# A complex-decay recurrence before a mixture of experts: TensorE adds the carried state to a chunk's state product, and the decays are kept in three places

## The chip, the cores and the metric

The kernel runs on one core of one Trainium2 chip. The metric is device time of one execution in microseconds (us), the median of the runs of the same program. A profile is one more execution, taken by the hardware profiler; its span, from the first to the last instruction, is somewhat shorter than its own time.

## The reference

Every (batch, head) has a complex state S of 48 x 48 that decays row by row with a complex factor and takes one outer product per token; the output of the recurrence goes through a top-1 mixture of experts with a capacity.

```python
mag = np.sqrt(a_re * a_re + a_im * a_im)
scale = np.minimum(mag, 0.999) / (mag + 1e-06)
a_re_n, a_im_n = (a_re * scale, a_im * scale)
for t in range(S):                       # S = 768, B = 4, H = 8, D = 48
    new_re = ar * S_re - ai * S_im
    new_im = ar * S_im + ai * S_re
    S_re, S_im = (new_re + kv, new_im)   # kv = k[t] (outer) v[t]
    y[:, :, t] = np.einsum('bhd,bhde->bhe', q[:, :, t], S_re)
x = y.transpose(0, 2, 1, 3).reshape(B * S, H * D)
# MoE: 3072 tokens, 8 experts, 384 -> 1024 (relu) -> 384, out = gate * expert(x)
```

## The kernel before, in words

**Tiling.** The 768 tokens are cut into 8 chunks of 96, the chunks into 4 groups of 2. Three kinds of work run through each other until the experts begin.

- *Slices.* A group has 6 slices of 8 decay factors. `norm_slice` (L370; `norm_first`, L285, for the very first) turns the raw decays into normalised ones; `scan` (L466) multiplies them up step by step on VectorE, a multiplication (L493) and an addition (L498) for each of 8 steps; `post` (L512) makes from the products the scaled q and k (`qko`, L541, L576) and sends them to HBM (`scr`, L584 to L598).
- *Units.* A unit is one batch b and one chunk c, 8 to a group, and it works one group behind the slices. It loads the scaled rows back (`qkc`, L684), transposes them (`tr`, L710), multiplies q by k (`pa`, L726), masks (`a_sb`, L730), and makes the output (`y`, L788 within the chunk, L793 from the carried state `z`). It also makes the state for the next chunk: the product k times v (`s`, L737 to L742, in the one PSUM tile `s_all`), the addition of the carried state z (`add`, L744), the multiplication by the chunk's decay (L759, L762, L765), and two accumulating DMAs that swap halves (`swap`, L753), after which the next chunk's z is there.
- *Routing.* The gate and the places of the tokens, and the sending of rows to the experts (L1133).

After the last unit's rows are placed, the experts run (`ph` L1374, `my` L1382, L1397).

**Decays.** A slice's tile `a4` has four places for each step: before the scan they hold r, -i, i, r. `mr` (L448) writes r into place 0 and `mi` (L444) writes i into place 2 on VectorE; `ci` (L451) copies i, negated, to place 1 and `cr` (L458) copies r to place 3 on ScalarE. The scan's multiplication reads all four places in a row, and its addition writes the running product into places 0 and 1. In the first slice of a group one step starts the product, so there `ci` is in two pieces.

**Order.** All of this is recorded as operations of a planner (`Plan.op`, L60). It holds a duration, an engine, the operations it follows, the buffers and a wished time for each, places them one by one (`solve`, L78), and the instructions of every engine are then written in that order. An engine works strictly in its order, so the order decides who waits. `fill_gaps` (L158) puts idle matmuls (`keep`, L225; they write other columns of `s_all`) into TensorE's planned gaps of over 0.4 us. The state product and its addition stand in the plan as:

```python
o = plan.op(K("S"), "PE", .8, s, w + SLATE * f, after=loaded + [K("LF"), K("V")], bufs=[("s", "u", b, c), R("qkc"), R("v")])
d = plan.op(K("D"), "DVE" if c else "ACT", dve(384) if c else act(384), add, w + (SLATE + 1) * f, after=[o] + zready, ...)
```

There is one `s` buffer: the next unit's state product waits until the addition has read this one.

Of the kernel before, what the change touches and what calls it, by code (L numbers as in the profile page):

```python
# [38 lines left out]
class Op:  # L39

    def __init__(self, eng, dur, fn, after, bufs, want, kb, idx):
        self.eng, self.dur, self.fn, self.after, self.bufs, self.want, self.kb, self.idx = eng, dur, fn, after, bufs, want, kb, idx
        self.lat = None
        self.start = None
        self.form = None
        self.begun = False


class Plan:
# [108 lines left out]
    def fill_gaps(self, keep, begin, stop, least=.4, one=.23):  # L158

        out, end = [], 0.  # L160
        for o in self.order:
            if o.eng == "PE":
                gap = o.start - end
                if begin < end and o.start < stop and gap > least:
# [3 lines left out]
                end = o.start + o.dur  # L168
            out.append(o)
# [11 lines left out]
class Att:  # L181
# [74 lines left out]
    def tile_a4(self, g, j):  # L256
        if (g, j) not in self.a4:
            self.a4[g, j] = self.p_a4.tile([128, SL, 4, D], F32, tag="a4", name=f"a4_{g}_{j}", bufs=RINGS["a4"])
        return self.a4[g, j]
# [25 lines left out]
    def norm_first(self, s0):  # L285
# [14 lines left out]
        for p, h in enumerate(range(n - HALF, -1, -HALF)):  # L300
# [13 lines left out]
            def xb(i=i):  # L314
                nc.vector.tensor_tensor(out=st['a4'][:, i, 3, :], in0=st['a4'][:, i, 0, :], in1=st['a4'][:, i, 1, :], op=ALU.add)

            def xc(i=i):
                nc.scalar.activation(st['ln'][:, i], st['a4'][:, i, 3, :], AF.Ln, bias=self.b_tiny)
# [9 lines left out]
            def mm(i=i):  # L328
                nc.vector.tensor_tensor(out=st['ln'][:, i], in0=st['a4'][:, i, 3, :], in1=st['ln'][:, i], op=ALU.mult)
# [14 lines left out]
            def mr(i=i):  # L344
                nc.vector.tensor_tensor(out=st['a4'][:, i, 0, :], in0=st['a'][:, 0, i], in1=st['t5'][:, i], op=ALU.mult)

            def ci(i=i, p=p):
                k = i.stop - (p == 0)
                nc.scalar.mul(out=st['a4'][:, i.start:k, 1, :], in_=st['a4'][:, i.start:k, 2, :], mul=-1.0)
                if p == 0:  # L350
                    nc.scalar.copy(out=st['a4'][:, k, 1, :], in_=st['a4'][:, k, 2, :])

            def cr(i=i):
                nc.scalar.copy(out=st['a4'][:, i, 3, :], in_=st['a4'][:, i, 0, :])  # L354
# [11 lines left out]
            orr = plan.op(None, "DVE", dve(m), mr, v + 7, after=[o], bufs=[a_, t5_, a4_])  # L366
            plan.op(K + ("i", p), "ACT", act(m) + .08 * (p == 0), ci, v + 7.5, after=[oi], bufs=[a4_])
            plan.op(K + ("r", p), "ACT", act(m), cr, v + 7.5, after=[orr], bufs=[a4_])

    def norm_slice(self, g, j, s0):  # L370
# [89 lines left out]
        oi = plan.op(None, "DVE", dve(n * D), mi, w + 10, after=[o], bufs=[a_, t5_, a4_])  # L460
        orr = plan.op(None, "DVE", dve(n * D), mr, w + 10.5, after=[o], bufs=[a_, t5_, a4_])
        plan.op(K + ("i",), "ACT", act(n * D) + .08 * (j == 0), ci, w + 11, after=[oi], bufs=[a4_])
        plan.op(K + ("r",), "ACT", act(n * D), cr, w + 11, after=[orr], bufs=[a4_])


    def scan(self, g, j, wants):  # L466
# [9 lines left out]
        for s in range(n - 1, -1, -1):  # L476
# [10 lines left out]
            def mul(cs, s=s, st=st, prev=prev):  # L487
# [1299 lines left out]
```

## Time and profile before

| | |
|---|---|
| median of 3 runs | 600.95 us (598.43 to 601.08) |
| profiled execution, its own time | 601.24 us |
| its span | 599.4 us |
| PE (TensorE matmul) busy | 530.0 us, 88% |
| DVE (VectorE) busy | 467.7 us, 78% |
| ACT (ScalarE) busy | 401.1 us, 67% |
| POOL (GpSimd) busy | 276.2 us, 46% |
| mean granted TensorE clock | 0.95 of full |

Shares are averages over two very different stages: slices and units up to some 366 us, and the experts from 372.6 us to the end, in which TensorE runs without a pause. Times of events are from the start of the span. A fp32 matmul stands in the trace as two records. A row's mean duration of one instruction is longer than what it takes of its engine, since the next one starts before it has ended; where work is dense the distance between two starts is what counts.

### The profile page before, as it was taken

Reading aid. Unit: us, or ns where it says so; the run is one execution under the profiler, and the core shown is the slowest. Engines: PE = TensorE matmul, PEld = TensorE weight load, DVE = VectorE, ACT = ScalarE, POOL = GpSimd, SP = SyncE. Lnnn points to the kernel's source line nnn. Section 1 sums busy time; section 2 is a strip of 40 time slices with the busy share of each in tenths; the row PEclk is TensorE's granted clock in tenths of the full one; section 3 lists DMA queues with packets and bytes.
Section 4 is the critical chain, followed back from the end, with each engine's and each line's share of the span. In section 5 each row is a group of like instructions: output and inputs, shape, how many; then the busy total and the mean of one; then the engine's idle time right before and its main releaser. Section 6 shows DMA issues by size and latency. Waiting matters only on the chain.

```text
span 599.4 us, 15649 instructions
## 1 busy us (share of the span) xinstructions
PE 530.0 (88%) x5453; PEld 460.3 (77%) x5453; DVE 467.7 (78%) x1388; ACT 401.1 (67%) x1115; POOL 276.2 (46%) x354
## 2 busy tenths in 40 slices
PE   2363879999999998999879998999999999999992
PEld 1131558777787776778768997999999999999991
DVE  5899979999899999999865668555797657567631
ACT  7656779998999889998564653345564746566430
POOL 9531414532457944476352722004554737355502
PEclk9667889999999999999997999999999999999997
DMA  5575797996898989879598972494745765884401
GB/s 172 179 192 159 179 225 179 266 235 164 207 233 202 233 240 227 219 195 204 139 183 191 252 197 48 72 228 140 168 128 127 213 152 174 189 206 139 128 19 39
DMA packets 90023, 105.51 MB, mean 176 GB/s; under 512 B 29846, under 2 KB 80495, under 8 KB 89936
## 3 DMA queue, kind: packets, MB, share of 16 engines
q1 hardware_dynamic: 72432, 57.27, 40.4%
q0 software_dynamic: 17504, 47.15, 29.9%
q8 instruction: 45, 0.74, 0.5%
q14 instruction: 42, 0.34, 0.2%
HBM read 71.41 MB, written 29.22 MB: 168 GB/s over the span
## 4 chain that ended last, share of the span: by engine, by line
PE 54%; ACT 18%; DVE 13%; DMA 8%; POOL 4%; issue 2%; POOLq 0%; SPq 0%; ACTq 0%; DVEq 0%
PE ph L1374 18%; PE my L1382 14%; PE my L1397 4%; ACT z L762 4%; PE pa L726 3%; DMA qkc<-scr 3%; DMA scr<-qko 3%; PE tr L710 2%; DVE xy L493 2%; PE y L788 2%; PE p L273 2%; PE n L273 2%; PE y L793 1%; DVE a L498 1%; DVE qko L576 1%
## 5 line engine op out<-in xcount | busy, mean ns | idle before, releaser
L1315 POOL DMA_INDIRECT out_dram<-oq,xr x66 | 69.5, 1054 | 61.4 <-ACT oq L1331 46.2
L1421 ACT ACTIVATE hh<-ph 128x448 fp32r<-128x448 f32 (+7 forms) x64 | 32.6, 510 | 96.6 <-PE ph L1374 96.6
L1422 DVE SCALAR_TENSOR_TENSOR hl<-ph,hh 128x448 fp32r<-128x448 f32 (+7 forms) x64 | 37.1, 580 | 66.5 <-ACT hh L1421 66.5
L1269 DVE TENSOR_TENSOR lo<-raw,hi 128x384 fp32r<-128x384 f32 (+2 forms) x128 | 65.4, 550 | 3.5 <-ACT hi L1268 3.2
L1374 PE MATMUL ph<-xh,hi 128*128 128x448 f32 (+7 forms) x192 | 67.3, 351 | 0.6 <-ACT xh L1227 0.6
L1374 PE MATMUL ph<-xh,lo 128*128 128x448 f32 (+7 forms) x192 | 67.2, 350 | 0.0
L1133 POOL DMA_INDIRECT disp<-x,idx x32 | 45.1, 1410 | 43.6 <-DVE a_sb L730 11.8
L755 POOL DMA_DIRECT2D z<-sx x56 | 47.4, 1060 | 31.6 <-ACT z L762 10.5
L493 DVE TENSOR_TENSOR xy<-a 128x192 f32<-128x192 f32 (+1 forms) x205 | 61.2, 313 | 0.6 <-ACT a L354 0.2
L710 PE MATMUL tr<-ident,qkc 81*96 81x81 f32 x512 | 54.0, 240 | 7.4 <-DMA qkc<-scr 4.1
L1268 ACT CAST hi<-raw 128x384 fp32r<-128x384 f32 (+2 forms) x128 | 58.9, 509 | 0.0
L273 PE MATMUL n<-a,ident 128*128 128x384 f32 x92 | 43.3, 604 | 16.8 <-ACT a L397 8.7
L726 PE MATMUL pa<-qT,kT 128*96 128x96 f32 x512 | 55.9, 255 | 0.8 <-ACT kT L714 0.8
L710 PEld LDWEIGHTS tr<-ident,qkc 81*96 81x96 f32 x512 | 41.6, 128 | 17.5 <-issue 5.5
L726 PEld LDWEIGHTS pa<-qT,kT 128*96 128x96 f32 x512 | 50.0, 169 | 2.8 <-ACT kT L714 1.4
L273 PE MATMUL p<-qko,ident 128*128 128x384 f32 x80 | 36.1, 580 | 16.5 <-ACT qko L530 16.4
L1382 PE MATMUL my<-hh,hi 128*128 128x448 f32 (+5 forms) x144 | 50.6, 351 | 0.0
L1382 PE MATMUL my<-hh,lo 128*128 128x448 f32 (+5 forms) x144 | 50.5, 351 | 0.0
L1382 PE MATMUL my<-hl,hi 128*128 128x448 f32 (+5 forms) x144 | 50.5, 351 | 0.0
L498 DVE TENSOR_TENSOR a<-xy 128x96 f32<-128x96 f32 (+1 forms) x221 | 49.1, 234 | 0.3
L730 DVE TENSOR_TENSOR a_sb<-pa,mask 96x384 f32<-96x384 f32 x64 | 34.9, 546 | 14.7 <-PE pa L726 14.6
L1374 PE MATMUL ph<-xl,hi 128*128 128x448 f32 (+7 forms) x192 | 46.2, 349 | 0.0
(248 smaller groups left out, 1442.6 us busy)
## 6 DMA issues: line engine op xcount, KB each, us to landing
qkc<-scr SPq DMA_DIRECT2D x32, 480.0 KB
raw<-in_moe_w_dram SPq DMA_DIRECT2D x128, 96.0 KB
raw<-in_moe_w_dram SPq DMA_DIRECT2D x32, 384.0 KB
scr<-qko POOLq DMA_DIRECT2D x44, 192.0 KB
scr<-qko POOLq DMA_DIRECT2D x20, 384.0 KB
a<-in_av_dram POOLq DMA_DIRECT2D x18, 384.0 KB
qkin<-in_xv_dram POOLq DMA_DIRECT2D x18, 384.0 KB
v<-in_vp_dram SPq DMA_DIRECT2D x32, 144.0 KB
```

The source lines that it names most:

```text
L273: nc.tensor.matmul(out=pt[:, :m], lhsT=self.ident, rhs=t[:, h:h + m], start=i == 0, stop=i == 1)
L493: nc.vector.tensor_tensor(out=st['xy'][:, :, cs].rearrange("p (u z) d -> p u z d", u=2), in0=a4[:, s, :, cs].rearrange("p (u z) d -> p u z ...
L498: nc.vector.tensor_tensor(out=self.a4[g, j][:, s, 0:2, cs], in0=xy[:, 0:4:2, cs], in1=xy[:, 1:4:2, cs], op=ALU.add)
L710: nc.tensor.transpose(out=pt[:, h * C:h * C + NE], in_=qk[:NE, 4 * hh + h, z_ * C:z_ * C + C], identity=self.ident[:NE, :NE])
L726: nc.tensor.matmul(out=pa[:, h * C:h * C + C], lhsT=kT[:, 4 * hh + h], rhs=qT[:, 4 * hh + h], start=True, stop=True)
L755: nc.gpsimd.dma_start(out=zn[a.start:a.stop or C], in_=st['sx'][o], accum_op=ALU.add)
L1133: ins = nc.gpsimd.indirect_dma_start(out=self.disp, out_offset=bass.IndirectOffsetOnAxis(ap=idx[:, c:c + 1], axis=0), in_=self.row(b, c0 + ...
L1268: return (lambda: nc.scalar.copy(out=h, in_=r), lambda: nc.vector.tensor_tensor(out=l, in0=r, in1=h.bitcast(F32), op=ALU.subtract))
L1269: lambda: nc.vector.tensor_tensor(out=l, in0=r, in1=h.bitcast(F32), op=ALU.subtract))
L1315: ins = nc.gpsimd.indirect_dma_start(out=out, out_offset=bass.IndirectOffsetOnAxis(ap=at, axis=0), in_=o, in_offset=None, bounds_check=las ...
L1374: nc.tensor.matmul(out=ph[:, :W], lhsT=a[:, k, fs], rhs=r[:, k, :W], start=i == 0, stop=i == len(parts) - 1)
L1382: nc.tensor.matmul(out=py[m][:, :W], lhsT=a[:, f % self.PF, ms], rhs=r[:, :W], start=f == 0 and i == 0, stop=f == NF - 1 and i == 2)
```

## The change

1. **State product.** For the units of chunks 1 to 5 (`summed`: 20 of the 28 units that make a state) TensorE leaves the product's accumulation open and a further matmul (`carry`) multiplies the carried z, 96 x 384, by the identity into the same PSUM tile. The sum is then only copied out, by ScalarE, where before VectorE added. Chunk 0 (copied by ScalarE before, too) and chunk 6 (added by VectorE) stay.
2. **No idle matmuls into an open sum.** `fill_gaps` puts none between a product and its carry.
3. **Three places.** `a4` holds -i, r, i. The multiplication reads (r, -i) and (i, r) out of them with a step of minus one place and writes the product over r and i. The copy `cr` is gone, and `ci` is in one piece. The readiness of a slice is that of `mr` and `ci`.

```diff
@@ Plan.fill_gaps
-                if begin < end and o.start < stop and gap > least:
+                if begin < end and o.start < stop and gap > least and not open_:
...
                 end = o.start + o.dur
+                open_ += o.opens
@@ tile_a4
-            self.a4[g, j] = self.p_a4.tile([128, SL, 4, D], F32, tag="a4", ...)
+            self.a4[g, j] = self.p_a4.tile([128, SL, 3, D], F32, tag="a4", ...)
@@ norm_slice (norm_first likewise)
-            nc.vector.tensor_tensor(out=self.a4[g, j][:, 0:n, 0, :], in0=st['a'][:, 0], in1=st['t5'], op=ALU.mult)
+            nc.vector.tensor_tensor(out=self.a4[g, j][:, 0:n, 1, :], in0=st['a'][:, 0], in1=st['t5'], op=ALU.mult)
         def ci():
-            a4 = self.a4[g, j]
-            k = n - (j == 0)
-            nc.scalar.mul(out=a4[:, 0:k, 1, :], in_=a4[:, 0:k, 2, :], mul=-1.0)
-            if j == 0:
-                nc.scalar.copy(out=a4[:, k, 1, :], in_=a4[:, k, 2, :])
-        def cr():
-            nc.scalar.copy(out=self.a4[g, j][:, 0:n, 3, :], in_=self.a4[g, j][:, 0:n, 0, :])
+            nc.scalar.mul(out=self.a4[g, j][:, 0:n, 0, :], in_=self.a4[g, j][:, 0:n, 2, :], mul=-1.0)
...
-        plan.op(K + ("r",), "ACT", act(n * D), cr, w + 11, after=[orr], bufs=[a4_])
+        plan.op(K + ("r",), "DVE", dve(n * D), mr, w + 10.5, after=[o], bufs=[a_, t5_, a4_])
@@ scan
-                w = self.a4[prev[0], prev[1]][:, prev[2], 0:2, cs]
+                w = self.a4[prev[0], prev[1]][:, prev[2], 1:3, cs]
...
+                a = a4[:, s, 1, cs]
+                a = bass.AP(a.tensor, a.offset, [a.ap[0], (D, 2), (-D, 2), a.ap[-1]])
                 nc.vector.tensor_tensor(out=st['xy'][:, :, cs].rearrange("p (u z) d -> p u z d", u=2),
-                                        in0=a4[:, s, :, cs].rearrange("p (u z) d -> p u z d", u=2), in1=w, op=ALU.mult)
+                                        in0=a, in1=w, op=ALU.mult)
@@ unit
-                                     start=True, stop=True)
+                                     start=h == 0 or not summed, stop=not summed)
+        summed = 0 < c and g < NG - 1
+        def carry():
+            nc.tensor.matmul(out=st['ps'], lhsT=self.ident[:, :C], rhs=z.rearrange("p h e -> p (h e)"), start=False, stop=True)
...
-            if c == 0:
+            if c == 0 or summed:
                 nc.scalar.copy(out=ss, in_=psv)
...
+            if summed:
+                o.opens = 1
+                o = plan.op(None, "PE", .68, carry, w + (SLATE + .5) * f, after=[o] + zready, bufs=[("s", "u", b, c), ("z", b, c)])
+                o.opens = -1
+            by = "DVE" if c and not summed else "ACT"
```

The planner places everything anew, so rows move on every engine. Two places matter to the prediction. The first is an inner unit, batch 2 of chunk 2. On VectorE, before, its addition (L751) stood among the slices' work (`a_2_3` is slice 3 of group 2, `qko_1`, `qko_2` are its slices 1 and 2, `sx` the state multiplied by a decay):

```order
L576 TENSOR_TENSOR qko_1_2393<-a_2_1_1724,v_2_1_2468 128x8x96
L449 TENSOR_TENSOR a_2_3_2174<-a_3_2004,t5n_3_2256 128x8x48
L1119 CAST idx_0_2559<-slot_0_2504 96x1
L751 TENSOR_TENSOR s_2_2660<-s_all,z_129 96x384
L765 TENSOR_TENSOR sx_1_1942<-s_1_1941,pcol_109 96x384
L765 TENSOR_TENSOR sx_2_2661<-s_2_2660,pcol_109 96x384
L493 TENSOR_TENSOR xy_3_7_2679<-a_2_3_2174,a_2_2_1916 128x192
```

VectorE has no such row any more for this unit (24 rows of this kind before, 4 after). TensorE now has, two transposes behind the unit's product (L730), the carry (L736):

```order
L1015 MATMUL x_1_2509<-ident,xt_1_2474 96x128 x4
L730 MATMUL s_all<-v_120,qkc_117 32x48 x24
L699 MATMUL tr_2_0_0_2550<-ident,qkc_117 96x81 x4
L699 MATMUL tr_2_1_0_2564<-ident,qkc_117 96x81 x4
L736 MATMUL s_all<-z_129,ident 96x384
L699 MATMUL tr_2_0_1_2575<-ident,qkc_117 96x81 x4
L699 MATMUL tr_2_1_1_2589<-ident,qkc_117 96x81 x4
```

and ScalarE the copy (L743), between two copies of transposed rows:

```order
L691 COPY qT_122<-ends_133 96x8x15
L743 COPY s_2_2586<-s_all 96x384
L703 COPY qT_122<-tr_2_0_1_2575 96x4x81
L703 COPY kT_124<-tr_2_1_1_2589 96x4x81
L519 ACTIVATE qko_2_2603<-a_2_2_1960 128x8x96
L756 ACTIVATE z_128<-s_2_2586,pcol_109 96x48 x8
```

The second place is on TensorE where the last group's units begin (batches 0 and 1 of chunk 6; `qkc_116` and `qkc_117` are their loaded rows, `y_6` the output of batch 0). Before:

```order
L710 MATMUL tr_6_1_1_4895<-ident,qkc_116 96x81 x4
L726 MATMUL pa_6_0_4903<-qT_122,kT_124 96x96 x4
L710 MATMUL tr_6_0_0_4920<-ident,qkc_117 96x81 x4
L726 MATMUL pa_6_1_4926<-qT_122,kT_124 96x96 x4
L710 MATMUL tr_6_1_0_4933<-ident,qkc_117 96x81 x4
L710 MATMUL tr_6_0_1_4940<-ident,qkc_117 96x81 x4
L788 MATMUL y_6_4946<-a_sb_126,v_119 64x96 x2
L793 MATMUL y_6_4946<-qT_122,z_128 48x96 x2
...
L741 MATMUL s_all<-v_119,qkc_116 32x48 x24
L710 MATMUL tr_6_1_1_4991<-ident,qkc_117 96x81 x4
```

Now:

```order
L699 MATMUL tr_6_1_1_4922<-ident,qkc_116 96x81 x4
L715 MATMUL pa_6_0_4928<-qT_122,kT_124 96x96 x4
L1015 MATMUL x_7_4936<-ident,xt_7_4903 96x128 x4
L715 MATMUL pa_6_1_4942<-qT_122,kT_124 96x96 x4
L730 MATMUL s_all<-v_119,qkc_116 32x48 x24
L699 MATMUL tr_6_0_0_4984<-ident,qkc_117 96x81 x4
L787 MATMUL y_6_4992<-a_sb_126,v_119 64x96 x2
L792 MATMUL y_6_4992<-qT_122,z_128 48x96 x2
```

The state product of batch 0, which needs the last rows loaded, moved ahead of three transposes of batch 1 and of the whole of batch 0's output. Idle matmuls (L227 before, L229 now) went from 90 to 64; from the first unit's transposes on they went from 61 to 25.

## Rows read from the trace of the kernel before

**Rows 1.** Stretches: length, busy us (count) of PE, PEld, DVE, ACT, POOL; clock, DMA share, GB/s.

```profile
100.00:150.00 50.00, 47.85 (x693) 37.88 (x692) 49.51 (x149) 47.05 (x138) 20.74 (x30) 1.00 0.90 222
150.00:200.00 50.00, 47.37 (x738) 38.19 (x738) 46.80 (x141) 48.81 (x157) 31.17 (x37) 1.00 0.87 215
...
sum 200.00, PE 190.35 PEld 152.71 DVE 190.93 ACT 180.41 POOL 108.77; mean PE 47.59 PEld 38.18 DVE 47.73 ACT 45.10 POOL 27.19
```

**Rows 2.** The same sums, 100 to 300 us, for L227, L751 and L459 alone.

```profile
sum 200.00, PE 16.67 PEld 13.78; mean PE 4.17 PEld 3.45
sum 200.00, DVE 10.36; mean DVE 2.59
sum 200.00, ACT 7.73; mean ACT 1.93
```

**Rows 3.** Groups of instructions: line, engine, operation, count, busy us, mean ns, idle before.

```profile
L751 DVE TENSOR_TENSOR s<-s_all,z 96x384 f32<-96x384 f32 x24 | 13.1, 546 | 7.0 <-PE s_all L741 5.8 <-DMA z<-sx 0.9 <-PE s_all L227 0.2
L459 ACT COPY a<-a 128x384 f32<-128x384 f32 x23 | 11.8, 513 | 0.4
L493 DVE TENSOR_TENSOR xy<-a 128x192 f32<-128x192 f32 x131 | 45.6, 348 | 0.5 <-ACT a L354 0.2
L493 DVE TENSOR_TENSOR xy<-a 128x96 f32<-128x96 f32 x74 | 15.6, 252 | 0.1
L493 DVE TENSOR_TENSOR xy<-a,a 128x192 f32<-128x192 f32 x19 | 6.6, 347 | 1.3 <-ACT a L459 1.2
```

**Rows 4.** VectorE in order of time at an addition: start, us.

```profile
305.86 0.55 DVE L751 TENSOR_TENSOR s<-s_all,z 96x384 f32<-96x384 f32 x1
306.32 0.38 DVE L1178 CAST number<-xr 96x448 fp32r<-96x448 int32 x1
```

**Rows 5.** ScalarE in order of time at chunk 0's copy and at a `cr`.

```profile
91.54 0.48 ACT L749 COPY s<-s_all 96x384 f32<-96x384 f32 x1
91.91 0.44 ACT L714 COPY qT<-tr 96x324 f32<-96x324 f32 x1
...
155.22 0.51 ACT L459 COPY a<-a 128x384 f32<-128x384 f32 x1
155.64 0.85 ACT L530 ACTIVATE qko<-a 128x768 f32<-128x768 f32 x1
```

**Rows 6.** TensorE in order of time: two 128x384 identity matmuls (four records), two groups of transposes.

```profile
175.50 1.50 PE L273 MATMUL n<-a,ident 128*128 128x384 f32 x4
176.83 0.72 PE L710 MATMUL tr<-ident,qkc 81*96 81x81 f32 x8
177.39 0.86 PE L726 MATMUL pa<-qT,kT 128*96 128x96 f32 x8
```

**Rows 7.** The chain that ended last, from the last slice's output on: start, us, what.

```profile
304.36 7.69 DMA scr<-qko
312.12 3.17 DMA qkc<-scr
315.33 1.50 PE s_all L741 x48
...
366.00 2.82 PE mt L1216 x14
...
372.64 2.50 PE ph L1374 x6
```

**Rows 8.** TensorE in order of time where the last group's units begin.

```profile
312.98 0.37 PE L793 MATMUL y<-qT,z 128*48 128x96 f32 x4 [1.60 <-DMA z<-sx]
...
315.33 1.50 PE L741 MATMUL s_all<-v,qkc 128*32 128x48 f32 x48 [0.99 <-DMA qkc<-scr]
...
322.87 0.88 PE L741 MATMUL s_all<-v,qkc 128*32 128x48 f32 x48
323.68 0.39 PE L788 MATMUL y<-a_sb,v 128*64 128x96 f32 x4
...
325.15 0.38 PE L1080 MATMUL pp<-oh,tri 96*96 96x64 f32 x2
```

More of the change, by code (lines that the diff above doesn't have):

```diff
@@ L46, in __init__ @@
         self.begun = False
+        self.opens = 0
 class Plan:
@@ L158, in fill_gaps @@
     def fill_gaps(self, keep, begin, stop, least=.4, one=.23):
-        out, end = [], 0.
+        out, end, open_ = [], 0., 0
         for o in self.order:
@@ L257, in tile_a4 @@
         if (g, j) not in self.a4:
-            self.a4[g, j] = self.p_a4.tile([128, SL, 4, D], F32, tag="a4", name=f"a4_{g}_{j}", bufs=RINGS["a4"])
+            self.a4[g, j] = self.p_a4.tile([128, SL, 3, D], F32, tag="a4", name=f"a4_{g}_{j}", bufs=RINGS["a4"])
         return self.a4[g, j]
@@ L314, in xb @@
             def xb(i=i):
-                nc.vector.tensor_tensor(out=st['a4'][:, i, 3, :], in0=st['a4'][:, i, 0, :], in1=st['a4'][:, i, 1, :], op=ALU.add)
+                nc.vector.tensor_tensor(out=st['a4'][:, i, 2, :], in0=st['a4'][:, i, 0, :], in1=st['a4'][:, i, 1, :], op=ALU.add)
             def xc(i=i):
-                nc.scalar.activation(st['ln'][:, i], st['a4'][:, i, 3, :], AF.Ln, bias=self.b_tiny)
+                nc.scalar.activation(st['ln'][:, i], st['a4'][:, i, 2, :], AF.Ln, bias=self.b_tiny)
             def xe(i=i):
@@ L328, in mm @@
             def mm(i=i):
-                nc.vector.tensor_tensor(out=st['ln'][:, i], in0=st['a4'][:, i, 3, :], in1=st['ln'][:, i], op=ALU.mult)
+                nc.vector.tensor_tensor(out=st['ln'][:, i], in0=st['a4'][:, i, 2, :], in1=st['ln'][:, i], op=ALU.mult)
             def tt(i=i):
@@ L344, in mr, with ci @@
             def mr(i=i):
[L345 to L354, printed above, removed]
+                nc.vector.tensor_tensor(out=st['a4'][:, i, 1, :], in0=st['a'][:, 0, i], in1=st['t5'][:, i], op=ALU.mult)
+            def ci(i=i):
+                nc.scalar.mul(out=st['a4'][:, i, 0, :], in_=st['a4'][:, i, 2, :], mul=-1.0)
             o = plan.op(K + ("load", p), "SP", .6, load, v - 14, bufs=[a_], kb=48 * HALF, extra=2.)
@@ L365, in norm_first @@
             oi = plan.op(None, "DVE", dve(m), mi, v + 7, after=[o], bufs=[a_, t5_, a4_])
-            orr = plan.op(None, "DVE", dve(m), mr, v + 7, after=[o], bufs=[a_, t5_, a4_])
-            plan.op(K + ("i", p), "ACT", act(m) + .08 * (p == 0), ci, v + 7.5, after=[oi], bufs=[a4_])
-            plan.op(K + ("r", p), "ACT", act(m), cr, v + 7.5, after=[orr], bufs=[a4_])
+            plan.op(K + ("r", p), "DVE", dve(m), mr, v + 7, after=[o], bufs=[a_, t5_, a4_])
+            plan.op(K + ("i", p), "ACT", act(m), ci, v + 7.5, after=[oi], bufs=[a4_])
     def norm_slice(self, g, j, s0):
@@ L448, in mr @@
         def mr():
[L449 removed]
+            nc.vector.tensor_tensor(out=self.a4[g, j][:, 0:n, 1, :], in0=st['a'][:, 0], in1=st['t5'], op=ALU.mult)
         def ci():
[L452 to L459 removed]
+            nc.scalar.mul(out=self.a4[g, j][:, 0:n, 0, :], in_=self.a4[g, j][:, 0:n, 2, :], mul=-1.0)
         oi = plan.op(None, "DVE", dve(n * D), mi, w + 10, after=[o], bufs=[a_, t5_, a4_])
[L461 to L463 removed]
+        plan.op(K + ("r",), "DVE", dve(n * D), mr, w + 10.5, after=[o], bufs=[a_, t5_, a4_])
+        plan.op(K + ("i",), "ACT", act(n * D), ci, w + 11, after=[oi], bufs=[a4_])
     def scan(self, g, j, wants):
@@ L527, in wa @@
         def wa():
-            st['w'] = self.a4[g, j][:, 0:n, 0:2, :]
+            st['w'] = self.a4[g, j][:, 0:n, 1:3, :]
             st['o'] = self.p_qk.tile([128, n, 2, 2, D], F32, tag="qko", name=f"qko_{g}_{j}", bufs=RINGS["qko"])
@@ L631, in grab @@
             pe = st['pe'] = self.pe[g]
-            w = self.a4[g, NS - 1][:, 0, 0:2, :]
+            w = self.a4[g, NS - 1][:, 0, 1:3, :]
             nc.scalar.copy(out=pe[:, :, 0, :], in_=w)
@@ L770, in unit @@
             o = plan.op(K("S"), "PE", .8, s, w + SLATE * f, after=loaded + [K("LF"), K("V")], bufs=[("s", "u", b, c), R("qkc"), R("v")])
-            d = plan.op(K("D"), "DVE" if c else "ACT", dve(384) if c else act(384), add, w + (SLATE + 1) * f, after=[o] + zready,
+            if summed:
[3 more added lines that the diff above has]
+            by = "DVE" if c and not summed else "ACT"
+            d = plan.op(K("D"), by, dve(384) if by == "DVE" else act(384), add, w + (SLATE + 1) * f, after=[o] + zready,
                         bufs=[("s", "u", b, c), R("s_sb"), R("sx")] + ([("z", b, c)] if c else []))
```

2 lines of the change are left out of this document (1 added, 1 removed).

## The prediction

> **What bounds the kernel now.** I read the busy time by stretch first, then the chain that ended last, then single rows in order of time. Two stages share the span. From 372.64 us the experts run on TensorE without a pause [rows 7]; nothing there is edited, so the question is when they start. That is set by the last group: its last slice is sent out (7.69 us) and read back (3.17 us), its first state product starts at 315.33 us, and from there the chain stays on TensorE until the rows for the experts are gathered at 366.00 us [rows 7]. So a gain has to come before 304 us, in the stage where slices and units share the engines.
>
> That stage has no single bottleneck. Between 100 and 300 us VectorE is busy 190.93 us of 200 (95.5%), TensorE 190.35, ScalarE 180.41 [rows 1]. From 150 to 200 us it is ScalarE that has most, 48.81 of 50 [rows 1]. But 16.67 us of TensorE's time are idle matmuls, put in to fill gaps [rows 2], so its real work is 173.7 us. VectorE is the fullest, with little between it and the others. TensorE runs at its full clock there, 1.00, that is 2.4 GHz [rows 1].
>
> **The change, part by part, between 100 and 300 us.**
>
> *The additions leave VectorE.* One takes 0.46 us of the engine (start at 305.86, the next at 306.32) [rows 4]. In the stretch there are 19 (10.36 us busy at 546 ns each) [rows 2, 3]; the twentieth is the one at 305.86. That takes off 19 x 0.46 = 8.7 us: VectorE falls to 182.2.
>
> *ScalarE trades one copy for another.* A `cr` takes 0.42 us (155.22 to 155.64) [rows 5]; 15 lie in the stretch (7.73 us at 513 ns) [rows 2, 3]: -6.3 us. The added copy has chunk 0's as its model, 0.37 us (91.54 to 91.91) [rows 5]: 20 times, +7.4 us. The second pieces of `ci` are a few tenths and left at nothing. ScalarE ends 1.1 us up, at 181.5. The `cr` removed before 100 us lie where the loads and not ScalarE set the pace; I count nothing for them. VectorE waited once, 1.2 us, for a `cr` to begin a slice [rows 3]; that wait is inside the idle share used below and is not counted again.
>
> *TensorE gets the carries.* The trace shows no matmul with z into an open sum; the nearest rows are the 128x384 identity matmuls, two in 1.33 us (175.50 to 176.83) [rows 6], so 0.665 us each. Twenty make 13.3 us: TensorE's real work rises from 173.7 to 187.0. What it loses are idle matmuls, 36 of the 61 that stood among the units, and they cost nothing while the real work keeps the clock up.
>
> *Does the carry wait for z?* TensorE would then hold everything behind it. In this trace the additions waited for z only once, 0.9 us of 24 [rows 3], and TensorE's y matmuls need the same z. I put this wait at nothing; it is the cover that would be lost if the swap DMAs came later.
>
> *The negative step.* The multiplication reads as many elements as before. It already read the carried pair twice over (a step of zero), and across a tile's border it takes 347 ns against 348 within a tile [rows 3]: how the operand lies shows in no row. I take 0; the upper end is a rival below.
>
> *The sum of the stage.* The fullest engine had 190.93 us of work; now it is TensorE with 187.0. At the same 95.5% the stage takes 187.0 / 0.955 = 195.9 us: **-4.1 us** at the last slice. The two ends: TensorE has room and VectorE's 182.2 us count, 182.2 / 0.955 = 190.8, **-9.2**; or TensorE keeps all it did not do (200 - 190.35 = 9.65 us of idling) and the idle matmuls left (25 of 61 of 16.67 = 6.8 us), 187.0 + 9.65 + 6.8 = 203.5, **+3.5**. I take -4.1, because TensorE's idle matmuls show that its gaps can be filled, but three engines at 91 to 94% cannot all be packed tighter than the fullest one was.
>
> **What is given back.** The output, its reading back and the state product behind it move forward with the last slice; their 11.0 us (304.36 to 315.33) stay [rows 7]. Before, TensorE did three groups of transposes and the whole output of batch 0 ahead of that state product, and still waited 1.60 us for z and 0.99 us for the rows [rows 8]. Now these stand behind it. They take 3 x 0.28 (two in 0.56 us) [rows 6] plus 1.47 us (323.68 to 325.15) [rows 8], 2.3 us, and from here the chain is TensorE's: **+2.3 us**. Zero would be the lower end (some wait further on takes it up), 4.6 the upper (all of it at the lower clock, next).
>
> **The clock.** Behind those waits the 48 records of a state product took 1.50 us where the same 48 took 0.88 us at 322.87 [rows 8]: TensorE had fallen to the lower of its two levels, 1.2 GHz, and was back before 322.87, so for up to 7.5 us. At half speed that costs at most 3.7 us. In the new order TensorE reaches the state product with less ahead of it, so it waits there at least as long, and I expect the same fall. If it stays at 2.4 GHz, up to 3.7 us are gained beside the sum; a longer fall costs as much.
>
> Sum: 601.24 (the profiled execution's own time) - 4.1 + 2.3 = 599.4 us. The median of the runs stands 0.29 us below the profiled execution, so **599.1 us**.
>
> **The rivals.**
>
> *TensorE has room.* For: VectorE was the fullest, and 16.67 us on TensorE were filler [rows 1, 2]. Against: without the filler it still gets to 187.0 us, more than either other engine. Then the stage gives 9.2: 600.95 - 9.2 + 2.3 = 594.0 us. The Trainium skill bears on this: Perfetto Trace Analysis, Identifying the Most-Contended Engine, says that matmul busy time is a poor measure of TensorE's headroom and names the busy share of the weight loads as one of two better ones. By that rule TensorE stood at 152.71 of 200 us, 76% [rows 1], had a quarter of its time free, and this rival would be the forecast; I weigh it less, since in these rows matmuls follow each other start to end and a carry's 0.665 us is streaming, not loading.
>
> *The transfers set the pace.* For: the DMA share is 0.87 to 0.90 in the two stretches shown, and the chain goes through 11 us of DMA [rows 1, 7]. Then the last slice ends where it did and the 2.3 us are paid: 603.2 us. Against: VectorE's additions waited for a transfer once, 0.9 us [rows 3].
>
> *TensorE becomes the queue that holds the others (slower).* It is strictly in order and now has two more points where it needs another engine: the carry needs z, and the next product needs ScalarE's copy to have read the only `s` buffer. It decides from the point where TensorE's waits and leftover idle matmuls exceed 200 - 187.0 = 13.0 us in this stretch; before they were 26.3 (9.65 and 16.67). At the upper end above: 600.95 + 3.5 + 2.3 = 606.7 us.
>
> *The negative step is slow.* If it doubled the time of an element: (348 - 252) / 96 = 1.0 ns each [rows 3], 192 in each of 188 multiplications, 36 us on VectorE, well over 620 us. The Trainium skill (Vector Engine (DVE) Microarchitecture Reference, Performance modes) lists an operand with a negative step among what was not measured, so it excludes nothing; no run here shows it yet either.
>
> That the change does not do what it says is excluded by the orders shown: 20 additions are gone from VectorE and 20 carries stand on TensorE.
>
> **How the numbers follow.** Forecast 0.50, TensorE with room 0.20, transfers 0.15, TensorE as the queue 0.12, the step 0.03. A measurement of this kernel tells about 0.5% from no change, 3.0 us: faster means below 597.95, slower above 603.95. The forecast's own spread (the clock, the order's 0 to 4.6) reaches from 595.5 to 602.5; I give 0.20 of its 0.50 to faster, 0.29 to same and 0.01 to slower. With the room's 0.20 faster is 0.40; with 0.14 of the transfers' same is 0.43; the rest, 0.17, is slower. The range runs from 594.0 (room) to 603.5 (transfers) and leaves out the queue and the step.
>
> **What would show it.** Right: the addition's rows on VectorE fall from 24 to 4; a carry takes about 0.67 us; VectorE's and ScalarE's busy time between 100 us and the last slice fall below TensorE's without filler; the last output leaves at about 300 us instead of 304.36; the first state product of the last group at about 311 us, after a wait of some us and at the lower clock; the experts start near 370.8 us. Wrong: L493's successor takes more than 350 ns; rows in which TensorE's carry waits for z or its product for ScalarE's copy, of over 5 us in sum; an output that leaves no earlier than 304 us; or a first state product that is not preceded by a wait.

## The result, and the profile after

The changed kernel takes 590.2 us (median of 6 runs, 589.29 to 590.69) against 599.69 us (596.76 to 605.47) for the kernel before beside it: ratio 0.9841, 95% interval 0.9806 to 0.9875. It is faster by about 9.5 us, where 1.85 were forecast, and lies below the range. The profiled executions took 601.24 and 590.26 us, their spans 599.4 and 588.4.

Five marks along the program tell where the 11.0 us of the spans come from. The first two are starts of an output multiplication on VectorE (`qko<-a,v`), of group 1's first slice and of the last slice.

| mark | before | after | lead | won since the mark above | forecast |
|---|---|---|---|---|---|
| output of group 1's first slice | 92.40 | 89.76 | 2.6 | 2.6 | 0 |
| output of the last slice | 303.11 | 294.60 | 8.5 | 5.9 | 4.1 |
| last group's first state product | 315.33 | 306.38 | 8.95 | 0.45 | 0 |
| the experts | 372.64 | 364.05 | 8.6 | -0.35 | -2.3 |
| end of the span | 599.4 | 588.4 | 11.0 | 2.4 | 0 |

The stretches, as [rows 1] has them for before:

```profile
100.00:150.00 50.00, 47.80 (x695) 36.62 (x693) 49.07 (x156) 46.69 (x142) 19.85 (x28) 1.00 0.94 234
...
sum 200.00, PE 193.70 PEld 151.89 DVE 191.35 ACT 184.51 POOL 102.99; mean PE 48.42 PEld 37.97 DVE 47.84 ACT 46.13 POOL 25.75
```

Equal times hold unequal work here, so the same work is better compared: from the first mark to the second, before and then after (columns as in [rows 1]), and after's idle matmuls in that stretch, which were 17.2 us before:

```profile
92.40:303.11 210.71, 201.06 (x3124) 161.43 (x3123) 201.57 (x608) 189.57 (x577) 112.72 (x133) 1.00 0.86 210
```

```profile
89.76:294.60 204.84, 198.79 (x3079) 156.29 (x3071) 196.16 (x652) 189.32 (x579) 105.71 (x133) 1.00 0.91 216
```

```profile
L229 PE MATMUL s_all<-ident 128*128 128x128 f32 x38 | 5.8, 286 | 0.3 <-ACT s L743 0.3
```

Without idle matmuls (the filler) TensorE went from 183.9 to 193.0 us. That is 9.1 us more, where 20 carries at 0.665 us would be 13.3; why its busy time grew by less is not shown. VectorE lost only 5.4 us, ScalarE nothing. VectorE stays the fullest. The groups of VectorE over the whole run (against [rows 3]) say why it lost so little:

```profile
L482 DVE TENSOR_TENSOR xy<-a 128x192 f32<-128x192 f32 x103 | 35.8, 347 | 0.1
L487 DVE TENSOR_TENSOR a<-xy 128x96 f32<-128x96 f32 x123 | 30.4, 247 | 0.1
L482 DVE TENSOR_TENSOR xy<-a 128x96 f32<-128x96 f32 x130 | 27.3, 251 | 0.0
L487 DVE TENSOR_TENSOR a<-xy 128x48 f32<-128x48 f32 x130 | 20.9, 201 | 0.0
L482 DVE TENSOR_TENSOR xy<-a,a 128x192 f32<-128x192 f32 x11 | 3.9, 353 | 0.6 <-ACT a L447 0.3
L482 DVE TENSOR_TENSOR xy<-a,a 128x96 f32<-128x96 f32 x18 | 3.8, 247 | 3.0 <-ACT a L447 2.9
L745 DVE TENSOR_TENSOR s<-s_all,z 96x384 f32<-96x384 f32 x4 | 2.2, 552 | 7.0 <-PE s_all L730 7.0
```

The additions fell from 24 to 4. But the planner now cuts more scan steps in two halves: 150 multiplications were whole and 76 halves, now it is 114 and 148. The scan's six rows sum to 122.1 us against 117.3 over the whole run. A multiplication with the negative step takes 347 ns against 348: the step costs nothing.

One carry in TensorE's order of time; it starts 0.65 us ahead of the next matmul, where 0.665 were forecast:

```profile
296.92 0.81 PE L736 MATMUL s_all<-z,ident 128*96 128x384 f32 x2
297.57 0.60 PE L599 MATMUL te<-ident,qko 128*96 128x128 f32 x4
```

**The hand-off to the first units**, TensorE in order of time, before and after:

```profile
76.38 2.17 PE L227 MATMUL s_all<-ident 128*128 128x128 f32 x18
82.28 0.96 PE L710 MATMUL tr<-ident,qkc 81*96 81x81 f32 x8 [3.72 <-DMA qkc<-scr]
83.03 2.85 PE L273 MATMUL n<-a,ident 128*128 128x384 f32 x4
```

```profile
76.41 2.84 PE L229 MATMUL s_all<-ident 128*128 128x128 f32 x24
80.68 1.56 PE L275 MATMUL n<-a,ident 128*128 128x384 f32 x4 [1.43 <-ACT a L392]
83.00 0.74 PE L699 MATMUL tr<-ident,qkc 81*96 81x81 f32 x8 [0.76 <-DMA qkc<-scr]
83.57 1.50 PE L275 MATMUL p<-qko,ident 128*128 128x384 f32 x4
```

Before, TensorE stood idle for 3.72 us until the rows read back had landed, and only then did `n`, a sum for a slice's norm. It did it at 1.2 GHz, in 2.85 us instead of 1.5. After, `n` stands ahead of the transposes and fills the wait, behind 12 idle matmuls instead of 9. The stretches from 80 to 88 us show the granted clock, before and after:

```profile
80.00:84.00 4.00, 1.72 (x10) 1.45 (x11) 3.58 (x12) 1.56 (x5) 0.70 (x1) 0.83 1.10 266
84.00:88.00 4.00, 4.00 (x22) 2.68 (x22) 0.68 (x3) 2.88 (x7) 0.72 (x2) 0.74 0.96 241
```

```profile
80.00:84.00 4.00, 2.56 (x14) 1.58 (x15) 4.00 (x17) 2.90 (x7) 0.23 (x1) 1.00 1.12 229
84.00:88.00 4.00, 3.86 (x39) 3.18 (x38) 3.34 (x17) 3.97 (x12) 1.19 (x2) 1.00 0.94 258
```

VectorE's first mask had waited for that; its row in order of time, before and after:

```profile
87.32 0.55 DVE L730 TENSOR_TENSOR a_sb<-pa,mask 96x384 f32<-96x384 f32 x1 [3.74 <-PE pa L726]
```

```profile
86.36 0.55 DVE L719 TENSOR_TENSOR a_sb<-pa,mask 96x384 f32<-96x384 f32 x1 [0.56 <-PE pa L715]
```

VectorE takes its work in order and stood at that mask: it was 0.68 us busy of 4 between 84 and 88 us, and 3.34 after, where more scan steps stand ahead of the mask.

**From the last output on**, the chain of after, answering to [rows 7]:

```profile
295.85 7.07 DMA scr<-qko
302.97 3.28 DMA qkc<-scr
306.38 0.88 PE s_all L730 x46
...
364.05 6.16 PE ph L1373 x27
```

TensorE there, answering to [rows 8]: the wait for the rows is longer than before, 3.08 us against 0.99, and the clock falls behind it. The transposes at 310.30 take 1.15 us instead of the 0.72 of [rows 6].

```profile
306.38 0.88 PE L730 MATMUL s_all<-v,qkc 128*32 128x48 f32 x48 [3.08 <-DMA qkc<-scr]
...
310.30 1.15 PE L699 MATMUL tr<-ident,qkc 81*96 81x81 f32 x8
```

**Where the experts begin**, a row of TensorE before and the 4 us of before, then the 4 us of after:

```profile
370.51 0.44 PE L1216 MATMUL mt<-number,rh 96*128 96x448 f32 x1 [1.41 <-DVE rs L1101]
```

```profile
372.00:376.00 4.00, 3.41 (x10) 2.97 (x10) 2.68 (x6) 1.58 (x3) 2.19 (x1) 0.60 0.02 5
```

```profile
364.00:368.00 4.00, 3.95 (x17) 3.08 (x18) 2.82 (x8) 1.56 (x3) 2.19 (x1) 1.00 0.13 38
```

Before, TensorE came to the experts behind a wait of 1.41 us for VectorE, and its clock was 0.60 there; after, no wait near them is longer than 0.6 us and the clock is 1.00. That is worth 1.2 of the 2.4 us: the 27 expert matmuls that come first took 7.16 us before and 6.00 after, and from the first to the end of the last it was 215.0 and 213.9 us. The other 1.2 us lie behind the last matmul, in the end of the program. The last pieces of the chain on TensorE, before and then after, end 11.7 and 10.5 us ahead of the end of the span (599.4 and 588.4):

```profile
582.72 4.95 PE my L1397 x27
```

```profile
572.97 4.95 PE my L1396 x27
```

In the runs below this end takes 11.7 us in every profile that has the additions on VectorE and the copies `cr` (f1, e3, e4, g1), 11.0 in those with the places alone (e1, g4) and 10.5 in those with the sum in TensorE. Why is not shown.

### The profile page after: what moved, and what is told of

It is laid out like the page before. It is cut to its first block, busy times and chain, and to the rows that moved or that the text cites. A ratio compares the mean times of both kernels' runs of the same rounds, so it can differ in the third digit from the quotient of the medians.

```text
span 588.4 us, 15673 instructions
## 1 busy us (share of the span) xinstructions
PE 529.3 (90%) x5441; PEld 456.0 (77%) x5441; DVE 463.2 (79%) x1436; ACT 397.7 (68%) x1106; POOL 268.5 (46%) x354
## 4 chain that ended last, share of the span: by engine, by line
PE 54%; DVE 18%; ACT 11%; DMA 8%; POOL 4%; issue 3%; POOLq 0%; SPq 0%; DVEq 0%; ACTq 0%
PE ph L1373 18%; PE my L1381 14%; PE my L1396 4%; PE pa L715 4%; DMA scr<-qko 3%; DVE xy L482 3%; PE tr L699 3%; ACT z L756 2%; DMA qkc<-scr 2%; DVE a L487 2%; PE y L787 2%; DVE qko L565 2%; DVE qko L530 2%; DMA z<-sx 2%; PE s_all L730 2%
## 5 line engine op out<-in xcount | busy, mean ns | idle before, releaser
L482 DVE TENSOR_TENSOR xy<-a 128x96 f32<-128x96 f32 (+1 forms) x233 | 63.1, 293 | 0.1
L275 PE MATMUL n<-a,ident 128*128 128x384 f32 x92 | 41.7, 586 | 19.9 <-ACT a L392 19.8
L699 PE MATMUL tr<-ident,qkc 81*96 81x81 f32 x512 | 52.7, 238 | 4.0 <-ACT ends L605 1.8
L715 PE MATMUL pa<-qT,kT 128*96 128x96 f32 x512 | 54.7, 251 | 0.4 <-ACT kT L703 0.3
L1132 POOL DMA_INDIRECT disp<-x,idx x32 | 37.0, 1157 | 37.9 <-DVE idx L1118 9.3
L487 DVE TENSOR_TENSOR a<-xy 128x96 f32<-128x96 f32 (+1 forms) x253 | 51.3, 223 | 0.1
L275 PEld LDWEIGHTS n<-a,ident 128*128 128x128 f32 x92 | 19.4, 225 | 33.6 <-ACT a L392 14.5
```

The lines of the kernel that those rows point to most:

```text
L275: nc.tensor.matmul(out=pt[:, :m], lhsT=self.ident, rhs=t[:, h:h + m], start=i == 0, stop=i == 1)
L487: nc.vector.tensor_tensor(out=self.a4[g, j][:, s, 1:3, cs], in0=xy[:, 0:4:2, cs], in1=xy[:, 1:4:2, cs], op=ALU.add)
L699: nc.tensor.transpose(out=pt[:, h * C:h * C + NE], in_=qk[:NE, 4 * hh + h, z_ * C:z_ * C + C], identity=self.ident[:NE, :NE])
L715: nc.tensor.matmul(out=pa[:, h * C:h * C + C], lhsT=kT[:, 4 * hh + h], rhs=qT[:, 4 * hh + h], start=True, stop=True)
```

## The experiments

Runs whose labels begin with the same letter ran on one chip, each letter on another chip. On two of the chips (e and h) the experts' stage was slower for every kernel (622.19 and 621.85 us for the kernel before), so a time is compared with a run on the same chip where there is one, and marks up to 310 us across chips.

**The two kernels again.** f1 and f2, without an edit.

> The kernel before, once more, for a like-for-like reading of the others of this call. Theory M (the change won about 3.3 us at the hand-off to the first units and 4 to 5 us in the stage of 100 to 300 us): the hand-off is as in the first profile, first transposes at 82.3 us after a wait of 3.7 us for the rows read back, VectorE's first mask after a wait of 3.7 us for TensorE, last output at about 303, first state product of the last group at about 315, experts at about 372. Rival L (the 3.3 us are only the chance of when one transfer lands): first transposes anywhere from 79 to 83 us and the experts' start moving with it, by up to 3 us.

> The changed kernel, once more. Theory M: first transposes at about 83.0 us after a wait under 1 us, the 128x384 matmul behind them 1.5 us and not 2.85, VectorE's first mask after 0.6 us, experts at about 364, 9 to 10 us under f1. Rival L: the wait before the first transposes varies as in f1, and the distance to f1 falls to 5 to 6 us when f1's transfer lands early.

f1: 601.6 us, profiled at 607.23; first transposes at 82.32 after 2.34 us, first mask after 4.60 us, experts at 378.33. f2: 589.26 us, ratio 0.9837 [0.9787, 0.9888]; first transposes at 82.48 after 0.27 us, `n` ahead of them, experts at 363.46. The hand-off is as in the first pair. What f1 adds is the spread: 10 us over 25 further runs of before on this chip (596.26 to 606.56), 2 over after's four. The profiled run of f1 is the longest of its ten, so it is read only for where the clock fell. It fell in more places than in the first profile:

```profile
84.00:88.00 4.00, 4.00 (x18) 2.84 (x17) 0.07 (x1) 2.69 (x7) 1.21 (x2) 0.50 0.90 214
...
312.00:316.00 4.00, 3.94 (x44) 3.68 (x45) 1.11 (x2) 1.48 (x5) 2.15 (x3) 0.74 1.02 192
...
324.00:360.00 36.00, 33.72 (x505) 30.91 (x502) 21.15 (x85) 18.89 (x55) 16.47 (x18) 0.91 0.90 217
```

**Each part alone.** The places without the sum (e1, g4: the changed kernel, edited) and the sum without the places (e2, h1: the kernel before with points 1 and 2 of the change, of which the plan's part is shown):

```diff
-        summed = 0 < c and g < NG - 1
+        summed = False
```

```diff
...
+            if summed:
+                o.opens = 1
+                o = plan.op(None, "PE", .68, carry, w + (SLATE + .5) * f, after=[o] + zready, bufs=[("s", "u", b, c), ("z", b, c)])
+                o.opens = -1
```

> The changed kernel without its carries: the decays lie in three places and the copies to the fourth are gone, but VectorE adds all 24 carried states as before. Theory M (two separate gains: about 3 us where the first units begin, because the new order keeps TensorE at 2.4 GHz there and puts VectorE's first mask later; about 5 us in the dense stage, from the additions that left VectorE): VectorE waits about 0.6 us for the first unit's pa, not 3.7; the dense stage gains little; 596 to 597 us where the kernel before has 600 and the change 590. Rival R (all of the gain comes from VectorE's freed 9 us; the first units are a symptom): 599 to 600 us. Both: the multiplication with the negative step takes 350 ns for 128x192, as before.

> The kernel before with the carries alone: four places and the fourth copy stay. Its idle matmuls ahead of the first units are the same as before (9 of them directly ahead). M: VectorE still waits about 3.7 us for the first unit's pa, and TensorE falls to 1.2 GHz there; the dense stage gains some 4 us; 595 to 597 us. R: 591 to 592 us.

> The changed kernel without the sum in TensorE: three places, negative step, no copies of the decays, but the additions on VectorE as before. Theory M: the planner's order at the hand-off comes with this part (n ahead of the transposes, no fall of the clock), so it takes 3 to 5 us of the 10.7 alone: 595.5 to 597.5. Rival R: the copies were on ScalarE, which was never the fullest engine, so at most 1 us: 599 to 600.

> The kernel before with the sum in TensorE alone (20 carries, 20 additions gone from VectorE, 20 copies added on ScalarE; four places and the copies of the decays as before). Theory J (in the stage of 100 to 300 us the two parts pay only together: without the copies of the decays removed, ScalarE takes 7.4 us more and is as full as VectorE was): from the first slice's output of group 1 to the last slice's output no time is won, last output 303 to 305, time 598 to 602. Rival S (the sum in TensorE alone wins the stage's 4 to 6 us, the places are worth only the hand-off): last output 298 to 300, time 594 to 597.

| | time | ratio | output of group 1's first slice | of the last | stage |
|---|---|---|---|---|---|
| before | | | 92.40 | 303.11 | 210.7 |
| e1 places | 614.94 | 0.992 [0.9885, 0.9955] | 89.66 | 301.19 | 211.5 |
| g4 places | 594.51 | 0.9875 [0.9833, 0.9917] | 89.17 | 302.32 | 213.2 |
| e2 sum | 618.54 | 0.9952 [0.9907, 0.9997] | 93.66 | 304.54 | 210.9 |
| h1 sum | 618.66 | 0.9975 [0.9936, 1.0013] | 92.08 | 304.17 | 212.1 |
| both | 590.2 | 0.9841 [0.9806, 0.9875] | 89.76 | 294.60 | 204.8 |

The ratios are to the kernel before on the same chip; the marks of "before" and "both" are those of the first pair. Neither part alone shortens the stage between the two marks; both together take 5.9 us off it in the first pair. Other profiles bear that out: the kernel before, and its variants that leave this stage as it was (f1, e3, e4, g1), have 210.1 to 211.4 us there, the changed kernel and its variants of that kind (f2, h3, i1, g2, g3, h4, i2) 204.7 to 207.2. The places bring the hand-off (2.7 to 3.2 us ahead, `n` ahead of the transposes) and, in both runs, a clock of 1.00 from 300 us into the experts; they alone save some 5 to 8 us. The sum alone brings little. The stage in e2:

```profile
93.66:304.54 210.88, 201.40 (x3057) 158.12 (x3056) 198.00 (x668) 193.24 (x595) 105.31 (x133) 1.00 0.86 210
```

VectorE is 3.6 us down, but ScalarE 3.7 up, since its new copies come with none taken away. In h1 it is the same (198.23 and 193.61), and the clock also fell twice in the stage (0.98). In e1 it is the other way round: ScalarE falls by 5.4 us, VectorE has all its work (202.44), and the stage does not move (211.5). In g4, with the same program, the clock fell once in the stage.

**Loads put on one engine** of the changed kernel. f3: a second matmul behind each carry, with zero weights, which closes the sum in the carry's place; f4: an addition of a scratch tile on VectorE at each of the 20 copies; h2: a copy of a scratch tile behind the `ci` of each slice but the very first, beside h3, the changed kernel again.

```diff
+            nc.tensor.matmul(out=st['ps'], lhsT=self.zero, rhs=z.rearrange("p h e -> p (h e)"), start=False, stop=True)
...
+                    nc.vector.tensor_tensor(out=self.junk[:C], in0=self.junk[:C], in1=self.junk[:C], op=ALU.add)
...
+            nc.scalar.copy(out=self.junk, in_=self.junk)
```

> The changed kernel with a second matmul of the carry's size (zero weights) behind each of the 20 carries: 20 x 0.66 = 13 us more on TensorE, nothing else. If TensorE is now what sets the stage (the forecast's step): +9 to +13 us. If it has room, its remaining idle time and idle matmuls taking it up (rival): 0 to +4 us.

> The changed kernel with a 96x384 addition of a scratch tile on VectorE at each of the 20 copies: 20 x 0.46 = 9 us more on VectorE, as much as the change took off. If VectorE's freed time is what the change gained (rival R): +7 to +9 us, nearly the whole gain lost. If TensorE sets the stage: 0 to +4 us.

> The changed kernel with a 128x384 copy of a scratch tile on ScalarE behind each slice's negation, that is the load of the removed copies of the decays back (some 0.42 us each, 15 of them between 100 and 300 us: 6.3 us). Theory J: the stage loses 4 to 6 us of what it won, time 593 to 596. Rival S (ScalarE's load does not matter): within 1 us of the changed kernel.

> The changed kernel again, for a like-for-like reading of the others of this call: 588.5 to 590.7, a spread under 3 us, where the kernel before has one of 7 us or more.

f3: 597.03 us, 7.8 above f2. f4: 596.61, 7.35 above f2. h2: 615.86, 6.05 above h3 (609.81 us; 608.23 to 610.14); between their profiles 1.4 us lie behind the experts' start, where the load is not. The stages of f3, f4, h2 and h3:

```profile
89.47:302.45 212.98, 208.96 (x3107) 162.19 (x3099) 197.77 (x651) 190.47 (x578) 105.67 (x133) 1.00 0.85 208
```

```profile
89.47:300.53 211.06, 200.55 (x3088) 156.42 (x3080) 204.49 (x671) 189.74 (x579) 106.19 (x133) 1.00 0.88 210
```

```profile
89.80:300.35 210.55, 201.67 (x3088) 157.28 (x3080) 197.01 (x652) 195.12 (x594) 105.85 (x133) 1.00 0.87 211
```

```profile
89.54:296.76 207.22, 200.76 (x3070) 158.21 (x3062) 196.56 (x651) 189.63 (x579) 106.00 (x133) 0.99 0.88 214
```

TensorE took 10.2 us more than in the first profile of after and the stage 8.1; VectorE 8.3 and 6.2; ScalarE 5.5 more than in h3 and 3.3. h3 has the longest stage of the changed kernel's profiles; against the others (204.7 to 206.0) ScalarE's load cost 4.6 to 5.8. So each load cost well over half of itself, on ScalarE at 92.7% busy too, and none was hidden. No engine has much room, and the fullest does not set the pace alone. The planner did not know of these loads, so a part of their price may be the place in the order where they stand and not how full the engine is; no run separates the two.

**The hand-off, undone and made.** e3: the kernel before with 16 more idle matmuls ahead of the first unit's transposes. g1: `n` ahead of them and three idle matmuls more, in the kernel before. g2: the same undone in the changed kernel. The parts of g1 and then g2 that place the steps:

```diff
...
+        at = order.index(turned)
+        order[at:at] = [Op("PE", 0, lambda: att.keep(3), [], [], 0, None, len(plan.ops) + 1), n3]
...
+        order[pe[here - 1]] = Op("PE", 0, lambda: att.keep(9), [], [], 0, None, len(plan.ops) + 1)
+        order.insert(pe[here + 2] + 1, n3)
```

> The kernel before with 16 more idle matmuls (3.7 us of them) on TensorE directly ahead of the first unit's transposes, where it waits for the loaded rows; nothing else differs. If the lower clock there is the cause: granted clock 1.00 from 80 to 88 us, the 128x384 matmuls there in 1.33 us and not 2.64, VectorE's wait for pa down from 3.7 to about 2 us, total 1.5 to 2.5 us shorter. If only the order of the rows matters: clock up, total the same within 0.5 us.

> The kernel before, with one step of TensorE moved: the sum n of slice 3 of group 1 ahead of the first unit's transposes instead of behind them, and three more idle matmuls ahead of it (12 instead of 9), as the changed kernel has it there. Theory M (at the hand-off the kernel before lets TensorE fall to 1.2 GHz in front of n, and VectorE waits for it; that is 3 us of the gain): clock 1.00 from 80 to 88 us, n in 1.5 us and not 2.85, VectorE's first mask after less than 1 us of wait, last output about 300, time 2 to 4 us under the kernel before. Rival R (the gain is all made in the stage of 100 to 300 us, by VectorE's freed time): the wait goes, but the stage behind takes it back; time within 1 us of before.

> The changed kernel with the same step put back: n of slice 3 behind the first two transposes, 9 idle matmuls instead of 12. Theory M: the clock falls to 1.2 GHz around 82 to 86 us, n takes 2.85 us, VectorE waits 3 to 4 us for its first mask, last output about 297 to 298 instead of 294.5, time 2 to 4 us above the changed kernel (589.3): 591 to 593. Rival R: no more than 1 us.

In g2 the fall is back (TensorE in order of time):

```profile
82.90 1.29 PE L699 MATMUL tr<-ident,qkc 81*96 81x81 f32 x8 [4.45 <-DMA qkc<-scr]
83.98 2.85 PE L275 MATMUL n<-a,ident 128*128 128x384 f32 x4
86.62 2.02 PE L275 MATMUL p<-qko,ident 128*128 128x384 f32 x4
```

VectorE's mask waits 4.26 us, group 1's first output comes at 93.49 instead of 89.76, the last at 299.21 instead of 294.60, and the kernel takes 592.47 us (591.97 to 594.49). That is 2.2 to 3.2 above the changed kernel's medians on three other chips, and 2.4 above g3, a variant of it on the same chip that wins nothing (below). By the ratio to the kernel before, 0.9859 [0.9818, 0.9901] against 0.9828 to 0.9841, it is 1 to 2 us, and the intervals overlap. In g1 the clock holds (1.00 from 80 to 88 us) and the mask comes at 84.52, 2.8 us earlier, but the first output only 1.6 earlier and the last 0.9; 601.09 us against 602.7, ratio 0.9998 [0.9968, 1.0029]. e3 also keeps the clock (last output 300.77) and also shows no gain: 622.07 us, ratio 1.0055 [1.0016, 1.0095]; its clock fell later, around 350 us. So undoing the step costs the changed kernel 4.6 us at the last output and some 1 to 3 at the end. Making it in the old kernel gains nothing in time.

**The clock at the last group.** e4: the kernel before with 7 idle matmuls ahead of its last-group `y` and 5 ahead of the state product. g3, h4 and i2: the changed kernel with 13 ahead of the state product; i1 is the changed kernel beside i2.

```diff
...
+            order.insert(at, Op("PE", 0, lambda: att.keep(k), [], [], 0, None, len(plan.ops) + 1))
...
+        idle(lambda o: o is plan.names["u", 0, 6, "S"], 13)
```

> The kernel before with 7 and 5 more idle matmuls on TensorE ahead of batch 0's output and its state product in the last group, where it waits 1.6 and 1.0 us. If the lower clock from 315 to 323 us costs what its rows show: the first state product's records take 0.88 us and not 1.50, and the experts start 2.5 to 3.7 us earlier, total about 597. If a later wait takes the gain up: experts start within 1 us of before.

> The changed kernel with 13 idle matmuls ahead of the last group's first state product, where TensorE waits about 3 us and comes back at 1.2 GHz for some 3.5 us. If those microseconds lie on the path: the clock stays at 1.00 from 300 to 330 us and the experts start 1.5 to 2 us earlier (362.3 instead of 364.0), time 587.3 to 587.8. If something else ends last there (a z or the rows): no change within 0.5 us.

> The changed kernel with 13 idle matmuls ahead of the last group's first state product, again, now beside the changed kernel on one chip. If the low clock behind that wait lies on the path: 1.5 to 2 us under h3. If it is taken up further on: within 0.7 us of h3.

> The changed kernel, for a like-for-like reading of i2: on an undisturbed chip 588.5 to 590.7, clock low for 3 to 4 us behind the first state product of the last group.

> The changed kernel with the 13 idle matmuls ahead of the last group's first state product. If the 1.6 us that the units behind it begin earlier in g3 (next state product 309.73 instead of 311.38) hold to the experts when no stall of instruction issue comes between: experts at about 362.4, median 1 to 2 us under i1. If not: within 0.7 us of i1, with the start taken up further on.

e4: 620.99 us, ratio 1.0029 [0.9994, 1.0064]. By itself the rows of its first unit landed early, transposes at 79.40 after 0.87 us; it was 3.6 us ahead of the first profile at the last output (299.52) and 0.45 at the experts (372.19; on another chip). g3: 590.04 us (588.26 to 593.25). h4: 611.62 against h3's 609.81. i2: 589.16 us (587.81 to 595.75) against i1's 590.29 (588.68 to 591.75); ratios 0.9829 and 0.9828. The idle matmuls keep the clock at that place, and in g3 the second state product begins 1.6 us earlier (309.73 instead of 311.38), but the experts do not begin earlier (365.45). A stall stands between:

```profile
326.46 0.27 PE L1028 MATMUL y<-xt,wg 128*32 128x96 f32 x1
328.49 0.37 PE L1028 MATMUL y<-xt,wg 128*32 128x96 f32 x7 [1.76 <-issue]
```

i2 has the same stall at L1028, of 2.0 us. Without its 1.76 us g3's experts would have begun at 363.69 at best, by this difference, 0.4 us ahead of the first profile, so the stall is not all that takes the lead back. No version beat the changed kernel clear of the noise.

## Why the prediction was wrong, step by step

**What the sum lacked.** It forecast 1.8 us (-4.1 and +2.3), and the spans differ by 11.0. Of the 9.2 us between, 2.6 lie ahead of group 1's first output and 2.4 behind the experts' start, two stretches that the sum put at nothing. Another 1.95 are the giving back that was hardly paid, 1.8 the stage, and 0.45 the sending out and reading back. No one term holds most of the miss.

**The stretch before 100 us: the step that failed first.** "The `cr` removed before 100 us lie where the loads and not ScalarE set the pace; I count nothing for them." What the copies' going did there was to change the order. With other costs the planner put `n` ahead of the first unit's transposes (e1 and g4, with the places alone, have it so), into a wait that was in the trace before with its 3.72 us and its clock of 0.83 and 0.74. The prediction's rows hold neither TensorE there nor that place in the new order. g2 undoes that step alone and loses 3.7 us at the first mark and 1 to 3 in all; g1 makes it in the old kernel and wins nothing in time, so its worth hangs on the order around it.

**The stage: right sign, size short, wrong reason.** 4.1 forecast, 5.9 measured in the first pair; seven more profiles with the same stage put it at 204.7 to 207.2 us, so one profile is uncertain by about 2 us. The price of a carry held (0.65 to 0.77 us to the next matmul where no wait follows, 0.665 forecast), as did that of the negative step (0), and no carry waited for z. What failed is the reason: "the fullest engine had 190.93 us of work; now it is TensorE". VectorE stayed fullest, 196.16 against TensorE's 193.0 without filler. It was cut by 5.4 instead of 8.7 us because of the split scan steps, which cost 3.8 us in this stage; they come with the sum (351 scan instructions in e2's stage, 271 in e1's, 270 before). At its old share (201.57 of 210.71, 95.7%) the measured VectorE work gives 196.16 / 0.957 = 205.0 us, which is the stage, and for e1 202.44 / 0.957 = 211.5, which is its stage too. But the same rule gives e2 198.00 / 0.957 = 206.9, and it took 210.9; so the fullest engine is not the whole answer. The loads point to all three being near their limit. The prediction booked ScalarE's two kinds of copies as a trade that nets to 1.1 us and touches nothing. By e2, and by h2's 3.3 us or more of stage for 5.5 us of copies, the copies that left are part of what let VectorE's relief pay. Why both parts together gain 5.9 and each alone nothing is shown as to loads only in part: each variant also has its own order, and what that is worth by itself was not separated.

**What is given back.** 2.3 forecast, 0.35 measured in the first pair. From the first state product to the experts it took 57.31 us before, 57.67 in after and 57.69 in f2, where the clock was low for some 4 us, and 58.69 in i1, where it was low for some 7, as before, and the first product took 1.50 us again. So at a like fall (i1) the moved work cost 1.4 us. Whether the shorter fall saved the rest in the first pair is not shown: the old order with a shorter fall (g1) took 57.33 us, no less than before. The term was right in kind and inside its bounds of 0 to 4.6.

**The clock.** "I expect the same fall" at the last group: it fell in after, f2 and i1, not in h3. The 2.4 us behind the experts' start were not in the sum at all. Half of them is the clock: the wait of 1.41 us for VectorE ahead of the experts, with a clock of 0.60 behind it, was in the trace and is gone in the new order. That the wait alone does not decide is shown by g1, which has it at the same length and keeps its clock; the experts' matmuls then take 213.8 us, as in after. The other half is the end of the program behind the last matmul, whose cause stays open.

**The rivals.** TensorE with room (594.0) came nearest in time, but fails by its mechanism: 10.2 us more on TensorE cost the stage 8.1. The Trainium skill (Perfetto Trace Analysis, Identifying the Most-Contended Engine) names the busy share of the weight loads as one of two measures of TensorE's headroom; by it a TensorE whose weight loads are busy 156.29 of 204.84 us, 76%, would have had a quarter of its time free, and f3 does not bear that out here. Transfers as the pace fail: the DMA share rose to 0.91 while the stage got shorter. TensorE as a queue fails: the carries waited for nothing, and among the state products only the last group's first one waited, for its rows. The negative step is excluded by 347 ns against 348.

## What to carry to other kernels

Where a planner sets the order from costs, a change of costs anywhere moves steps everywhere: read the new order at every wait of the old trace, also far from the edit, and price the waits that a moved step can fill, with the clock that falls behind them. Where three engines are all at 90% or more, ask what lands on the others when the fullest is freed; here the copies taken from ScalarE and the additions taken from VectorE paid only together. Take a second and a third profile before you read anything from 2 us between two marks: the kernel before scattered by 10 us from run to run and its clock fell in other places from profile to profile, and the changed kernel scattered by 1 to 3. What narrowed the scatter was not isolated.

## What the runs showed of the hardware

TensorE's clock did not fall behind every wait of the same kind: at the last group's 3.08 us of wait for its rows it was low for some 4 us (after), at 2.79 for some 7 (i1), at 2.77 not at all (h3), with the same program. Behind 1.41 us ahead of the experts it was 0.60 over 4 us in before and stayed at full speed in g1. The rows read back for the first unit landed between 79.4 and 82.3 us in runs of the same early program (e4, first profile). Stalls of TensorE of 1.3 to 2.0 us that the profile puts down to instruction issue came in six runs at one place each (e2, g3, g4, h2, h3, i2); in g3 and i2, which have the same program, both at L1028. In h4, which has that program too, none came there. Their cause is not shown.
